# A fused attention and two-layer MoE kernel: token blocks of 512 in place of 384, and other places in SBUF for the buffers around them

## The chip, the cores and the metric

The kernel runs on one core of a Trainium2 chip. The metric is the device time of one execution in microseconds (us), taken as the median of several runs. Engines are named as the profile names them: PE is TensorE (PEld its weight loads), DVE is VectorE, ACT is ScalarE, POOL is GpSimd, SP is SyncE, which here issues every DMA; SPq, ACTq and so on are the engines' instruction queues.

## The reference

Three stages follow each other; their tensors come in as 64-bit or 32-bit floats, and the output is 32-bit. The MoE weights come in as 64-bit floats and are turned into 32-bit floats on the chip.

```python
# 1: chunked attention, q, k, v of 4 x 8 x 768 x 64, 8 memory keys per head
for c in range(nc):                      # chunks of 32 queries
    q_c = q[:, :, c_start:c_end]
    k_ctx = k[:, :, l_start:r_end]       # 16 keys to the left, 8 to the right
    k_full = np.concatenate([mem_k, k_ctx], axis=2)
    v_full = np.concatenate([mem_v, v_ctx], axis=2)
    scores = scale * np.matmul(q_c, k_full.transpose(0, 1, 3, 2))
    a = softmax(scores)
    out[:, :, c_start:c_end] = np.matmul(a, v_full)
x = out.transpose(0, 2, 1, 3).reshape(3072, 512)
# 2: first MoE, w_gate and w_val 512 x 1536, w_out 1536 x 512
x = (sigmoid(x @ w_gate) * (x @ w_val)) @ w_out
# 3: second MoE, w_in 512 x 2048, w_out 2048 x 512
h = x @ w_in
y = (h * sigmoid(1.702 * h)) @ w_out
```

## The kernel before

**Numbers as two halves.** Every matmul operand is split into a high part (rounded to the matmul's format) and a low part (the remainder), and each product is three matmuls: high by high, high by low, low by high. A weight slot `w` holds both parts of one unit of weights (128 x 2 x 512), and x is held as `xh` and `xl`.

**Blocks and phases.** The 3072 tokens go in 8 blocks of 384. Phase 1 runs the first MoE over each block: for each of 12 slices f of the hidden layer, `first_product` multiplies x by a gate slice (8 matmuls with the high weights, L694, and 4 with the low, L701), then by a value slice; `gated` makes the sigmoid on ACT (L718), the product on DVE (L721), and its high and low parts `gh` (ACT, L724) and `gl` (L728); `gemm2` multiplies them by an output slice into four PSUM banks Y (12 matmuls, L845). That is 36 matmuls, each 128 x 128 by 128 x 384, for a block and an f. The result goes to DRAM (`y_dram`) through two staging tiles and comes back for phase 2, the second MoE: per block and f of 16, 12 matmuls 384 wide (L694, L701) and 9 that are 512 wide (`gemm4` through `mm3`, L672), since there the weights are the moving operand and the output has 128 tokens a tile (3 tiles a block).

**Attention.** Each of 32 tiles covers 96 queries, so a block holds exactly four. The tiles of block 0 come first, the prologue, all PE-path (q, k and the probabilities are transposed on PE, L357, L365, L564; scores L474, values L625; evicted into `xh` by ACT, L635, and `xl` by DVE, L639); those of block 1 are PE-path tiles that run inside block 0, in one set of buffers `pa`; the others run inside the block before their own (`attention_b`), with transposes on DVE (L458 to L464, L599) from q and k that many small DMAs bring in (L283).

**Conversion.** One unit of 64-bit weights (512 KB) goes through `convert`: a DMA into a buffer `raw` (L240), ACT `rebias` (L244), DVE `rest` (L249), ACT `sign` (L254), DVE `join` (L257), ACT `high` (L262), POOL `low` (L266). 36 units belong to phase 1 and are converted during the prologue and block 0, 32 to phase 2 and are converted in slots of phase 1 as those come free, from block 7 on. There are 3 raw buffers, and 2 more for the first 16 units in the place of the second x block. 17 slots lie where the prologue's buffers were.

**Order.** `Schedule` lists every step with its engine, an assumed duration, what it reads and writes and a due time, and sets the order of the instructions of each engine by it; `clock` gives the matmuls' due times. On the chip each engine then works strictly in that order and waits at an instruction whose inputs are not there. PE has one gate bank G and one value bank V, so the gate product of f+1 cannot begin before ACT has read the sigmoid of f out of G.

Of the kernel before, what the change touches and what calls it, by code (L numbers as in the profile page):

```python
# [130 lines left out]
def kernel(  # L131
# [40 lines left out]
    clock = [20.0]  # L172
# [13 lines left out]
    NXR = 16  # L186
# [13 lines left out]
    def xkeys(i):  # L200
        return [("x", i, c) for c in range(BLK // TQ)]
# [25 lines left out]
    def convert(slot, src, late=False):  # L227
        u = nconv[0]
        nconv[0] += 1
        i = nraw[0]  # L230
# [793 lines left out]
```

## Time and profile before

| | us |
|---|---|
| median of 3 runs | 1271.63 (1267.9 to 1279.07) |
| the profiled execution | 1272.78 |
| its span, first to last instruction | 1270.9 |
| PE busy | 1225.8 (96%), 8320 matmuls |
| DVE, ACT, POOL busy | 612.1, 532.3, 219.4 |

The profiled execution is 1.9 us longer than its span. Busy time of PE is modelled from start to the end of the pipeline, so neighbouring matmuls overlap in it, and the time that a stream of matmuls takes is read from the distance of their starts.

### The profile page before, as it was taken

To read this page: it belongs to the slowest core of one execution; us is meant where nothing else is said; L and a number is where in the kernel's file an instruction comes from. 1 tells how busy PE (TensorE), PEld (TensorE's weight loads), DVE (VectorE), ACT (ScalarE), POOL (GpSimd) and SP (SyncE) were. 2 spreads that over 40 slices of the span, in tenths; PEclk is the share of its full clock that TensorE was granted. 3 is DMA by queue.
4 is the path that set the end of the run, shared out by engine and by line. 5 is a ranking of instruction groups with operands and counts; after the bars stand their busy time and mean duration, and the time that the engine had idled before them with its cause. 6 is when DMAs were issued, how large, how long until landed. Compare 5 with 4: busy or idle time off the path is not lost.

```text
span 1270.9 us, 20929 instructions
## 1 busy us (share of the span) xinstructions
PE 1225.8 (96%) x8320; PEld 1149.7 (90%) x8320; DVE 612.1 (48%) x1274; ACT 532.3 (42%) x902; POOL 219.4 (17%) x202
## 2 busy tenths in 40 slices
PE   5698899999999999999999999999999999999998
PEld 4688799899999999999999989999999999998997
DVE  6775757647738467385555631222222222222322
ACT  4998824333424234243358962323232322222222
POOL 3575600000000000000046662101010000001000
PEclk8899999999999999999999999999999999999999
DMA  9646433322303123021034520101010101010000
GB/s 189 181 140 181 136 57 66 64 82 44 71 15 52 47 40 72 12 48 49 18 104 165 176 91 1 50 1 50 1 50 1 50 1 38 13 36 15 26 1 26
DMA packets 173213, 78.04 MB, mean 61 GB/s; under 512 B 137659, under 2 KB 166587, under 8 KB 173115
## 3 DMA queue, kind: packets, MB, share of 16 engines
q1 hardware_dynamic: 173115, 76.71, 23.1%
q8 instruction: 65, 1.06, 0.3%
q14 instruction: 33, 0.27, 0.1%
HBM read 64.08 MB, written 12.58 MB: 60 GB/s over the span
## 4 chain that ended last, share of the span: by engine, by line
PE 77%; ACT 8%; SPq 4%; DMA 4%; DVE 4%; issue 2%; POOL 2%; ACTq 0%; DVEq 0%; POOLq 0%
PE bank L694 28%; PE bank L672 21%; PE bank L701 14%; PE bank L845 11%; SPq L283 4%; ACT raw L254 3%; ACT f L244 2%; PE bank L625 2%; DVE f L257 1%; DMA raw<-in_moe_w_val_dram 1%; DMA raw<-in_moe_w_out_dram 1%; PE bank L474 1%; POOL w L266 1%; DVE raw L249 1%; ACT w L262 1%
## 5 line engine op out<-in xcount | busy, mean ns | idle before, releaser
L694 PE MATMUL bank<-xh,w 128*128 128x384 f32 x1280 | 437.6, 342 | 20.6 <-ACT sig L718 14.2
L694 PE MATMUL bank<-xl,w 128*128 128x384 f32 x1280 | 434.6, 340 | 1.3 <-DVE xl L639 1.3
L721 DVE TENSOR_TENSOR sig<-bank,sig 128x384 f32<-128x384 f32 x224 | 124.4, 555 | 416.8 <-ACT sig L718 312.0
L701 PE MATMUL bank<-xh,w 128*128 128x384 f32 x1280 | 276.2, 338 | 0.4 <-POOL w L266 0.4
L718 ACT ACTIVATE sig<-bank 128x384 f32<-128x384 f32 x224 | 110.9, 495 | 387.4 <-PE bank L701 386.8
L694 PEld LDWEIGHTS bank<-xh,w 128*128 128x128 f32 x1280 | 243.8, 190 | 28.1 <-ACT sig L718 16.7
L694 PEld LDWEIGHTS bank<-xl,w 128*128 128x128 f32 x1280 | 244.1, 191 | 3.8 <-DVE xl L639 1.8
L672 PE MATMUL bank<-w,gh 128*128 128x512 f32 x768 | 239.2, 393 | 0.0
L701 PEld LDWEIGHTS bank<-xh,w 128*128 128x128 f32 x1280 | 227.1, 188 | 9.3 <-POOL w L266 0.7
L724 ACT ACTIVATE gh<-sig 128x384 fp32r<-128x384 f32 x224 | 117.7, 525 | 174.5 <-DVE sig L721 167.3
L845 PE MATMUL bank<-gh,w 128*128 128x384 f32 x768 | 166.2, 338 | 2.1 <-ACT f L868 1.6
L672 PEld LDWEIGHTS bank<-w,gh 128*128 128x128 f32 x768 | 142.1, 188 | 21.7
L672 PE MATMUL bank<-w,gl 128*128 128x512 f32 x384 | 151.3, 394 | 0.0
L728 DVE TENSOR_TENSOR gl<-sig,gh 128x384 fp32r<-128x384 f32 x184 | 104.2, 566 | 94.2 <-ACT gh L724 92.3
L845 PEld LDWEIGHTS bank<-gh,w 128*128 128x128 f32 x768 | 135.6, 188 | 4.5 <-ACT f L868 2.0
L266 POOL TENSOR_TENSOR w<-f,w 128x512 fp32r<-128x512 f32 x68 | 93.4, 1381 | 67.0 <-ACT w L262 63.9
L542 POOL TENSOR_TENSOR pn_b<-e,sm 96x448 f32<-96x448 f32 x24 | 23.2, 968 | 457.3 <-DVE sm L534 457.3
L894 POOL TENSOR_TENSOR xl<-f,xh 128x384 fp32r<-128x384 f32 x32 | 33.2, 1040 | 339.8 <-ACT xh L891 339.6
L254 ACT ACTIVATE raw<-raw 128x512 f16<-128x512 f32 x62 | 84.4, 1379 | 9.0 <-DVE raw L249 8.8
L672 PEld LDWEIGHTS bank<-w,gl 128*128 128x128 f32 x384 | 72.2, 188 | 17.2 <-DVE gl L728 0.3
L599 DVE STREAM_TRANSPOSE pt<-pn_b 32x256 f32<-32x256 f32 x192 | 83.6, 435 | 3.0
L845 PE MATMUL bank<-gl,w 128*128 128x384 f32 x384 | 82.5, 336 | 0.2 <-POOL gl L728 0.2
(79 smaller groups left out, 869.2 us busy)
## 6 DMA issues: line engine op xcount, KB each, us to landing
raw<-in_moe_w_out_dram SPq DMA_DIRECT2D x26, 512.0 KB
raw<-in_moe_w_in_dram SPq DMA_DIRECT2D x16, 512.0 KB
y_dram<-f SPq DMA_DIRECT2D x32, 192.0 KB
f<-y_dram SPq DMA_DIRECT2D x32, 192.0 KB
out_dram<-f SPq DMA_DIRECT2D x23, 256.0 KB
vn<-in_v_dram SPq DMA_DIRECT2D x24, 240.0 KB
raw<-in_moe_w_gate_dram SPq DMA_DIRECT2D x10, 512.0 KB
raw<-in_moe_w_val_dram SPq DMA_DIRECT2D x10, 512.0 KB
```

Of the source, the lines that this page charges most:

```text
L254: nc.scalar.activation(half[:, :, 1], words[:, :, 1].bitcast(F32), AF.Copy, scale=2.0**-60)
L266: nc.gpsimd.tensor_tensor(out=w[:, 1, :], in0=ft, in1=w[:, 0, :].bitcast(F32), op=ALU.subtract)
L283: add("sp", 0.45, lambda: nc.sync.dma_start(out=dst(), in_=src), r=list(r), w=[key], nbytes=n)
L599: nc.vector.transpose(T["pt"][r * CH : (r + 1) * CH, :, c * CH : (c + 1) * CH], T["pn"][c * CH : (c + 1) * CH, :, kb * CH : (kb + 1) * CH],)
L672: nc.tensor.matmul(ps_out, a, c, start=(first and i == 0 and j == 0), stop=(last and i == n - 1 and j == 2),)
L694: nc.tensor.matmul(bank[bk][:, :n], w[:, 0, ts[t]], x[xb][:, t, :n], start=t == 0 and x is xhs, stop=False)
L701: nc.tensor.matmul(bank[bk][:, :n], w[:, 1, ts[t]], xhs[xb][:, t, :n], start=False, stop=t == NK - 1)
L718: nc.scalar.activation(sig[:, :n], bank[src_sig][:, :n], AF.Sigmoid, scale=scale)
L721: nc.vector.tensor_tensor(out=sig[:, :n], in0=bank[src_val][:, :n], in1=sig[:, :n], op=ALU.mult)
L724: nc.scalar.activation(gh[:, :n], sig[:, :n], AF.Copy)
L728: eng.tensor_tensor(out=gl[:, :n], in0=sig[:, :n], in1=gh[:, :n].bitcast(F32), op=ALU.subtract)
L845: nc.tensor.matmul(bank[Y[m]][:, :n], w[:, wi, m * P : (m + 1) * P], g[:, :n], start=f == 0 and j == 0, stop=f == F1 - 1 and j == 2,)
```

## The change

Blocks have 512 tokens, so there are 6. A tile of 96 no longer divides a block: `tiles[b]` lists the tiles that begin in block b (6, 5, 5, 6, 5, 5), and a tile that lies in two blocks is evicted in two parts; of tiles 5 and 10 the second part is held back (`held_back`) until the next x block can be written. The prologue has 6 tiles in place of 4, block 0 carries 5 PE-path tiles in place of 4, and blocks 1 to 4 carry 21 in place of 24. Each matmul of phase 1, and each `first_product` of phase 2, is 512 wide; phase 1 has 36 x 12 x 6 matmuls in place of 36 x 12 x 8, phase 2 has 24 x 16 x 6 (all 512 wide) in place of 21 x 16 x 8, 4896 in place of 6144. Phase 2 uses 4 of 6 output banks for a block, in a ring, where it had two sets of 3.

In the conversion, every second unit's sign is made on DVE (`sign_dve`) and not on ACT. The first 8 units have 5 raw buffers (the two of the second x block), units 8 to 29 have 5 as well (two lie in slots that are filled last), then 3. 26 slots lie where the prologue was. The four slots filled last hold those two raw buffers and the buffers of `pa` first: units 34 and 35 (output slices 10 and 11) can be written only when the last PE-path tile, tile 10, has been transposed. `attention_b` has no buffers of its own: k lies in `raw0` and `raw1`, the unnormed probabilities in `raw2`, q and the memory keys in `f0` and `f1`, so its loads wait for the last conversions of block 0, and those of phase 2's weights wait for the last attention tile.

```diff
-    BLK = 384
-    blocks = [4] * 8
+    BLK = 512
+    NB = NT // BLK
+    tiles = [[t for t in range(NTILE) if t * TQ // BLK == b] for b in range(NB)]
+    NPRO = len(tiles[0])
+    NPE = NPRO + len(tiles[1])
...
-    clock = [20.0]
+    clock = [34.0]
...
-    NXR = 16
+    NXR = 8
+    NSR = 30
...
-    NLATE = 17
+    NLATE = 26
...
+        more = (NRAW, NRAW + 1) if u < NXR else (NRAW + 2, NRAW + 3) if u < NSR else ()
+        at = (*range(NRAW), *more)
+        i = at[nraw[0] % len(at)]
...
+        def sign_dve():
+            half = bits().bitcast(U16).rearrange("p (c w) -> p c w", w=4)
+            nc.vector.tensor_scalar(
+                out=half[:, :, 1], in0=half[:, :, 3], scalar1=0x8000, scalar2=None, op0=ALU.bitwise_and
+            )
...
-        add("act", c_act(512), sign, r=[kr], w=[kr2])
+        if u % 2:
+            add("dve", 0.9, sign_dve, r=[kr], w=[kr2])
+        else:
+            add("act", 1.4, sign, r=[kr], w=[kr2])
...
+            for i, blk in enumerate(sorted({c // NCH for c in g})):
+                if part not in (None, i):
+                    continue
+                cs = [c for c in g if c // NCH == blk]
+                a = (cs[0] - g[0]) * CH
+                m = len(cs) * CH
...
-            evict()
+            if t not in (NPRO - 1, NPE - 1):
+                evict()
+            else:
+
+                evict(0)
+                held_back.append(lambda: evict(1))
...
+        new_slots(late_pool[0], [u[1] for u in order[NW - NLATE : NW - 4]])
+        sraw.extend(spare(i, [P, 512], I64, f"raw_s{i}") for i in (3, 2))
+        t = spare(1, [P, 2, H, D], F32, "qkn_a")
+        pa.t.update(qn=t[:TQ, 0], kn=t[:, 1], pw=spare(0, [TQ, H, P], F32, "pw_a"))
...
+        kb = [blocks4(raw[i].bitcast(F32), 2 * NCK + 1) for i in range(2)]
+        qb = [blocks4(fts[i], NCK) for i in range(2)]
+        mn, mt = [fts[i][:, NP * TQ :].rearrange("p (a r) -> p a r", a=NP) for i in range(2)]
+        pn = raw[2].bitcast(F32)[:TQ, : H * 3 * CH].rearrange("s (h k) -> s h k", h=H)
...
+        if u == NW - 2:
+            add("none", 0.0, lambda: open_slots((1, 0)), w=named(pa) + ["ident_a", "pa"])
+            gate = "pa"
+        convert(s, src, gate)
+    conv_keys = bits_keys(range(NRAW)) + [("f", i) for i in range(NF)]
+    add("none", 0.0, open_pb, w=conv_keys + ["pb"])
...
-    O = [[Y[0], Y[1], Y[2]], [Y[3], A0, A1]]
+    ring6 = [*Y, A0, A1]
+    O = [[ring6[(TT * b + i) % 6] for i in range(TT)] for b in range(NB)]
...
+        if b == 0:
+            held_back.pop()()
```

Line numbers of the changed kernel differ (L694 becomes L726, L718 becomes L750, and so on). How the instructions stand is shown at three places.

**ACT in block 0**, some four units of conversion, before (L244 is `rebias`, L254 `sign`, L262 `high`, L724 `gh`):

```order
L244 ACTIVATE f3_80<-raw2_76 128x512
L254 ACTIVATE raw2_76<-raw2_76 128x512
L244 ACTIVATE f2_79<-raw0_74 128x512
L254 ACTIVATE raw0_74<-raw0_74 128x512
L262 ACTIVATE w15_107<-f1_78 128x512
L262 ACTIVATE w25_105<-f3_80 128x512
L724 ACTIVATE gh1_84<-sig1_82 128x384
L262 ACTIVATE w26_108<-f2_79 128x512
L254 ACTIVATE xh1_raw_89<-xh1_raw_89 128x512
```

and after (L257 is `rebias`, L267 `sign`, L281 `high`, L756 `gh`):

```order
L281 ACTIVATE w3_106<-f0_77 128x512
L257 ACTIVATE f1_78<-raw_s2_655 128x512
L267 ACTIVATE raw0_74<-raw0_74 128x512
L595 ACTIVATE pt_97<-bank2_68 128x384
L281 ACTIVATE w15_107<-f1_78 128x512
L257 ACTIVATE f2_79<-raw0_74 128x512
L756 ACTIVATE gh0_83<-sig0_81 128x512
L257 ACTIVATE f3_80<-raw1_75 128x512
L267 ACTIVATE raw2_76<-raw2_76 128x512
```

Before, a sign stands beside each `rebias`; after, every second unit has none on ACT.

**DVE at the end of block 0**, before, from the last x tile of block 1 (`xl1`, L639) to the transposes of the first `attention_b` tile (L461, L462):

```order
L639 TENSOR_TENSOR xl1_783<-bank3_69,xh1_782 128x4x96
L721 TENSOR_TENSOR sig1_82<-bank1_67,sig1_82 128x384
L257 SCALAR_TENSOR_TENSOR f0_77<-f0_77,raw0_74 128x512
L249 TENSOR_SCALAR raw1_75<-raw1_75 128x512
L257 SCALAR_TENSOR_TENSOR f1_78<-f1_78,raw1_75 128x512
L438 STREAM_TRANSPOSE mt_b_1498<-mn_b_1497 128x128
L721 TENSOR_TENSOR sig0_81<-bank1_67,sig0_81 128x384
L728 TENSOR_TENSOR gl0_85<-sig0_81,gh0_83 128x384
L866 COPY f3_80<-bank5_71 128x384
L721 TENSOR_TENSOR sig1_82<-bank1_67,sig1_82 128x384
L866 COPY f3_80<-bank7_73 128x384
L461 STREAM_TRANSPOSE kt_93<-kbkb_0_1494 128x12x32
```

and after (L593 is the copy of tile 10's probabilities, L482 to L485 and L479 the transposes and copies of the first `attention_b` tile from `raw1` and `f1`, L675 the eviction into `xl`, L753 the product with the sigmoid, L918 the eviction of the Y banks into the staging tile `f3`):

```order
L593 COPY pt_97<-bank3_69 128x384
L482 STREAM_TRANSPOSE kt_93<-raw1_75 128x12x32
L483 STREAM_TRANSPOSE kt_93<-raw1_75 128x12x32
L485 COPY kt_93<-f1_78 128x4x8 x3
L675 TENSOR_TENSOR xl1_725<-bank3_69,xh1_724 128x4x64
L675 TENSOR_TENSOR xl0_88<-bank3_69,xh0_87 128x4x32
L479 STREAM_TRANSPOSE qt_92<-f1_78 128x384
L753 TENSOR_TENSOR sig0_81<-bank1_67,sig0_81 128x512
L760 TENSOR_TENSOR gl0_85<-sig0_81,gh0_83 128x512
L918 COPY f3_80<-bank5_71 128x512
L918 COPY f3_80<-bank7_73 128x512
L753 TENSOR_TENSOR sig1_82<-bank1_67,sig1_82 128x512
```

The transposes from freshly loaded k and q have moved ahead of the last `xl` of block 1 and ahead of the Y evictions.

**SP at the same place**, before (L240 loads weights, L872 stores block 0's result):

```order
L240 DMA raw1_75<-in_moe2_w_out_dram 128x512
L283 DMA qbqb_0_1493<-in_q_dram 32x4x32 x3
L283 DMA mn_b_1497<-in_mem_k_dram 8x4x32 x4
L283 DMA kbkb_0_1494<-in_k_dram 32x6x32 x16
L283 DMA kbkb_0_1494<-in_k_dram 16x4x32
L872 DMA y_dram_65<-f2_79 128x384
```

and after (L253 loads weights, L924 stores):

```order
L253 DMA raw2_76<-in_moe_w_out_dram 128x512
L305 DMA vn_91<-in_v_dram 120x8x64
L305 DMA vn_91<-in_mem_v_dram 8x8x64
L305 DMA f1_78<-in_q_dram 32x4x32
L305 DMA f0_77<-in_mem_k_dram 8x4x32 x4
L305 DMA raw1_75<-in_k_dram 32x4x32 x16
L305 DMA f1_78<-in_q_dram 32x4x32 x11
L305 DMA raw0_74<-in_k_dram 32x7x32 x16
L305 DMA vn_91<-in_v_dram 120x8x64
L305 DMA f0_77<-in_q_dram 32x4x32 x10
L924 DMA y_dram_65<-f2_79 128x512
```

The first store of a block's result has moved from behind 17 k loads to behind two sets of 16 and two sets of q loads.

## Rows read from the trace of the kernel before

**Rows 1.** Busy time by stretches: start:end, length, busy us (instructions) per engine, PEclk, DMA.

```profile
0.00:35.90 35.90, 21.24 (x321) 17.86 (x321) 23.66 (x52) 17.95 (x37) 10.65 (x19) 0.81 0.82 174
13.50:36.20 22.70, 14.31 (x201) 11.96 (x200) 20.41 (x45) 12.49 (x24) 8.45 (x12) 0.70 0.71 183
35.90:155.70 119.80, 100.65 (x752) 92.76 (x753) 86.33 (x126) 112.15 (x166) 77.48 (x65) 0.93 0.57 166
155.70:650.30 494.60, 492.93 (x4131) 480.64 (x4131) 304.90 (x775) 172.09 (x283) 26.18 (x29) 1.00 0.23 48
650.30:731.90 81.60, 78.49 (x445) 76.62 (x444) 48.58 (x64) 69.72 (x104) 52.93 (x41) 1.00 0.53 174
731.90:1270.90 539.00, 532.52 (x2677) 481.82 (x2675) 148.64 (x259) 160.36 (x315) 52.20 (x50) 1.00 0.08 26
```

**Rows 2.** Instruction groups of PE from 35.9 to 155.7 us: count, busy, mean, idle before.

```profile
L694 PE MATMUL bank<-xh,w 128*128 128x384 f32 x100 | 39.3, 393 | 15.4 <-ACT sig L718 11.6 <-ACT w L262 3.8
L694 PE MATMUL bank<-xl,w 128*128 128x384 f32 x100 | 37.9, 379 | 1.3 <-DVE xl L639 1.3
L701 PE MATMUL bank<-xh,w 128*128 128x384 f32 x100 | 23.1, 355 | 0.4 <-POOL w L266 0.4
L845 PE MATMUL bank<-gh,w 128*128 128x384 f32 x88 | 18.9, 342 | 0.0
L845 PE MATMUL bank<-gl,w 128*128 128x384 f32 x44 | 9.7, 341 | 0.2 <-POOL gl L728 0.2
L564 PE MATMUL bank<-ident_a,pw_a 96*128 96x96 f32 x32 | 3.8, 268 | 1.8 <-POOL pw_a L542 1.8
L625 PE MATMUL bank<-pt,vn 128*64 128x96 f32 x64 | 3.5, 252 | 0.3 <-ACT pt L574 0.3
L474 PE MATMUL bank<-kt,qt 64*32 64x64 f32 x192 | 2.9, 221 | 1.1 <-ACT qt L372 1.1
L365 PE MATMUL bank<-ident_a,kn_a 128*128 128x128 f32 x16 | 2.4, 272 | 0.0
L357 PE MATMUL bank<-ident_a,qn_a 96*128 96x96 f32 x16 | 2.0, 245 | 0.0
```

**Rows 3.** Timeline of PE: start us, us, engine, line; three places in turn.

```profile
605.49 0.34 PE L694 MATMUL bank<-xh,w 128*128 128x384 f32 x1
...
611.73 0.34 PE L694 MATMUL bank<-xh,w 128*128 128x384 f32 x1
...
842.70 0.63 PE L672 MATMUL bank<-w,gh 128*128 128x512 f32 x2
...
844.78 0.51 PE L701 MATMUL bank<-xh,w 128*128 128x384 f32 x2
...
45.55 0.53 PE L694 MATMUL bank<-xh,w 128*128 128x384 f32 x1
45.87 0.53 PE L694 MATMUL bank<-xl,w 128*128 128x384 f32 x1
```

**Rows 4.** Conversion: groups of 35.9 to 155.7 us; L249's line view, ns min/median/max.

```profile
L254 ACT ACTIVATE raw<-raw 128x512 f16<-128x512 f32 x30 | 40.9, 1384 | 3.0 <-DVE raw L249 3.0
...
L249 DVE TENSOR_SCALAR raw<-raw 128x512 int32<-128x512 int32 x30 | 26.9, 904 | 7.1 <-DMA raw<-in_moe_w_gate_dram 2.5 <-DMA raw<-in_moe_w_val_dram 2.3 <-DMA raw<-in_moe_w_in_dram 2.1
...
L249 DVE TENSOR_SCALAR xh_raw<-xh_raw 128x512 int32<-128x512 int32 x3 | 3.9, 1301 | 0.0
...
L249 DVE TENSOR_SCALAR raw<-raw x62: 407/629/1974, 31.2 to 740.2; 128x512 int32<-128x512 int32 x62
```

**Rows 5.** Attention's groups on PE from 155.7 to 650.3 us, of 24 tiles.

```profile
L625 PE MATMUL bank<-pt,vn 128*64 128x96 f32 x384 | 21.1, 252 | 0.0
L474 PE MATMUL bank<-kt,qt 64*32 64x64 f32 x1152 | 17.7, 221 | 0.0
```

**Rows 6.** The first-product group of PE from 650.3 to 745 us.

```profile
L694 PE MATMUL bank<-xh,w 128*128 128x384 f32 x112 | 38.2, 341 | 5.3 <-ACT sig L718 2.7 <-DVE sig L721 2.6
```

**Rows 7.** Timeline of SP's queue at the start of block 1.

```profile
151.75 9.31 SPq L283 DMA_DIRECT2D kbkb<-in_k_dram  x17
161.49 0.83 SPq L872 DMA_DIRECT2D y_dram<-f  x2
```

More of the change, by code (lines that the diff above doesn't have):

```diff
@@ L795 @@
-    for i, (_, s, src) in enumerate(order[: NW - NLATE]):
-        convert(s, src)
-        if i == 0:
-            for t in range(NPRO):
-                attention(t, pro_bufs[t], pro_banks[t], True)
-    used = []
-    for x in pro_bufs:
-        for n in x.t:
-            used += [(x.k[n], i) for i in range(4)] + [x.k[n]]
-    add("none", 0.0, open_late, w=used + ["ident", "late"])
-    for _, s, src in order[NW - NLATE :]:
-        convert(s, src, True)
-    add("none", 0.0, open_x1, w=["x1"] + [k for i in range(2) for k in (("raw", NRAW + i), ("raw", NRAW + i, 2))])
@@ L808 @@
[L808 to L813 removed]
+        late_pool.append(ctx.enter_context(tc.tile_pool(name="cp2", bufs=1)))
+        new_slots(late_pool[0], [u[1] for u in order[NW - NLATE : NW - 4]])
+        sraw.extend(spare(i, [P, 512], I64, f"raw_s{i}") for i in (3, 2))
+        t = spare(1, [P, 2, H, D], F32, "qkn_a")
@@ new lines, in named, with bits_keys, attend @@
+    def named(bufs):
+        return [k for n in bufs.k for k in [(bufs.k[n], i) for i in range(4)] + [bufs.k[n]]]
+    def bits_keys(ids):
+        return [("raw", i, *x) for i in ids for x in ((), (2,))]
+    def attend(ts, bufs, banks):
+        for t in ts:
+            attention(t, bufs(t), banks(t), True)
+    gate = None
+    for u, (_, s, src) in enumerate(order):
+        if u == 1:
+            attend(tiles[0], lambda t: pro_bufs[t], lambda t: pro_banks[t])
+        if u == NXR:
+            add("none", 0.0, open_late, w=[k for x in pro_bufs for k in named(x)] + ["ident", "late"])
+            add("none", 0.0, open_x1, w=["x1"] + bits_keys((NRAW, NRAW + 1)))
+            held_back.pop()()
+            attend(tiles[1], lambda t: pa, lambda t: (A0, A1))
+            gate = "late"
+        if u == NW - 4:
+            add("none", 0.0, lambda: open_slots((3, 2)), w=["sraw"] + bits_keys((NRAW + 2, NRAW + 3)))
+            gate = "sraw"
+        if u == NW - 2:
+            add("none", 0.0, lambda: open_slots((1, 0)), w=named(pa) + ["ident_a", "pa"])
+            gate = "pa"
+        convert(s, src, gate)
@@ L831, in attention_b @@
     def attention_b(b):
-        for t in range(tile0[b], tile0[b] + blocks[b]):
+        for t in tiles[b]:
             first = t == NPE
@@ L896, in lo @@
                 )
-            add("sp", 0.45, load, r=[("y", m, NTB * b + i) for i in range(NTB)], w=[kst], nbytes=P * BLK * 4)
+            add("sp", 0.45, load, r=[("y", m, b)], w=[kst], nbytes=P * BLK * 4)
             add("act", c_act(BLK), hi, r=[kst], w=xkeys(xb))
@@ L927 @@
     freed.sort()
+    quads = range(0, P, CH)
+    done = [(f"kb{i}", r, p) for i in range(2) for r in quads for p in (0, 1, 2, 3, "edge")]
+    done += [(f"qb{i}", r, c) for i in range(2) for r in quads for c in range(NCK)]
+    done += [("mn", r) for r in quads] + ["mt", ("pn", 0), ("pn", 1), "pb"]
+    add("none", 0.0, lambda: None, w=done + conv_keys)
     slot_in2 = [freed[2 * f][1] for f in range(F2)]
```

128 lines of the change are left out of this document (58 added, 70 removed).

## The prediction

> **What bounds the kernel now.** I first cut the span at the places where the work changes and read the busy times by stretch [rows 1]: the prologue up to the first matmul of the first product (35.9 us), block 0 up to the end of block 1's first gate product (155.7), blocks 1 to 6 (650.3), the last block of phase 1 (731.9) and phase 2. From 155.7 on PE is busy for 492.9 of 494.6, 78.5 of 81.6 and 532.5 of 539.0 us: the other engines are covered there. Ahead of that it is not: 21.2 of 35.9 us in the prologue and 100.7 of 119.8 in block 0, at a mean granted clock of 0.81 and 0.93, while ACT is busy for 112.2 of the 119.8. So the kernel is PE for 1115 us, and ACT's conversion and DVE's attention for the first 156.
>
> In block 0 I counted what PE does [rows 2]: 432 matmuls of the products and four PE-path tiles, which together were busy for 14.6 us, 3.65 a tile (an upper bound, since neighbours overlap in it). The pace of a product matmul is read from starts [rows 3]: from 605.49 to 611.73 lie 36 of 384 columns, 173.3 ns each. So block 0 holds 432 x 0.1733 = 74.9 + 14.6 = 89.5 us of work in 119.8, and **30.3 us are lost**. The same rows give 20.5 us of idle time, of which 16.8 ended with ACT (15.4 ahead of the first product, 1.1 and 0.3 ahead of scores and values); the clock took 0.07 x 119.8 = 8.4, and some 1.4 is left for restarts.
>
> **The wider matmul itself: nothing.** From 842.70 to 844.78 lie 9 matmuls of 512 columns, 231.1 ns each; 231.1 / 173.3 = 1.333 is just 512 / 384 [rows 3]. At 45.55 us two of 384 columns are 0.32 us apart [rows 3], which is 384 / 1.2 GHz, the lower of the two clock levels, with nothing beside it. So the columns are paid, and the 1248 matmuls that fall away (6144 to 4896) were not paid singly. Phase 1 is 3456 x 0.1733 = 599 us before and 2592 x 0.2311 = 599 after; phase 2 is 1536 x 0.1733 + 1152 x 0.2311 = 532.4 before and 2304 x 0.2311 = 532.5 after. The Trainium skill, on the page "TensorE: Matmul & The Clock Gate", section "Back-to-back issue gap", has a gap of N / 2.4 + 2.5 ns when warm, a fixed 2.5 ns for each matmul. By it, as an estimate, 1248 fewer would save 3 us; the rows are 6.6 to 7.1% above its 162.5 and 215.8 ns and show no fixed part, so the sum takes none.
>
> **The prologue: +11.4 us.** It has six tiles in place of four. DVE sets its pace: 20.4 of 22.7 us busy from 13.5 to 36.2 [rows 1], for four tiles less the first maximum, with a few conversion steps among them. A tile costs 20.4 / 4 = 5.1 by busy time, 22.7 / 4 = 5.7 by elapsed time, and 35.9 / 4 = 9.0 if the opening loads counted for each; two more are 10.2 to 18 us. I take the elapsed 11.4, since loads of later tiles run beside earlier ones: first product at 47.3. The two more memsets lie in DVE's wait for the first loads.
>
> **Block 0: work 118.1 us, loss 7.4 in place of 30.3.** PE's work becomes 432 x 0.2311 = 99.8 + 5 x 3.65 = 18.3, together 118.1. Against that stands the supply:
> - ACT was busy for 112.2 us, 41.5 of it in 30 signs of 1384 ns [rows 4]. Half of these go: 20.8. The remaining 70.7 either stay or, at most, grow by a quarter with the fifth tile and with 512 columns: 91 to 109 us. Both ends are below 118.1, so ACT no longer bounds the block.
> - DVE was busy for 86.3 us [rows 1]. It gets 15 signs. No row shows that instruction; the nearest is L249, also one in-place operation on every second word of the same buffer, at 407 ns at least, 904 in the mean of this stretch, 1974 at most [rows 4]. The signs cost 6 to 30 us; I take the mean, 13.6. With the rest unchanged or, without L249's 26.9, a quarter larger, DVE comes to 100 to 115 us: also below 118.1, though not by much.
> - Raw buffers are five in place of three for units 16 to 29, so DVE's 7.1 us of waiting for weights [rows 4] shrinks; that is cover, not gain.
>
> With ACT below PE, I let the 16.8 us of waits that ended with ACT go and keep the other 3.7; the clock's loss was 8.4 for 20.5 us of idle time, so 3.7 leave 1.7. To this come 2 us at the end of the block, which did not stand there before: DVE now has the transposes of freshly loaded k ahead of the last `xl` of block 1, and 17 such loads took SP 9.3 us to issue [rows 7]. By the order they begin when the last value slice's low part is done on POOL, some 50 product matmuls ahead of the end (11.6 us), and land about when DVE comes to them. The sum is 3.7 + 1.7 + 2 = 7.4; the bounds are 2 and the present 30.3. Block 1's first gate product ends at 47.3 + 118.1 + 7.4 = **172.8** in place of 155.7.
>
> **The rest: 1115.2 us becomes 1082.3.** Block 0 has done 512 tokens and not 384, so phase 1 has 2160 matmuls of 0.2311 left in place of 3024 of 0.1733: 499.2 for 524.1, -24.9. Three attention tiles fewer are left, each (21.1 + 17.7) / 24 = 1.6 us on PE [rows 5]: -4.9. In the turn to phase 2 PE waited 5.3 us [rows 6], on ACT and DVE busy with the second conversion (ACT 69.7 of 81.6 us [rows 1]). A block and its weights' slots now last a third longer for the same 32 units, and ACT has half the signs; I take 3 of the 5.3 off, with 0 and 5.3 as ends. Phase 2 stays, and so does the tail. The output ring costs nothing: the banks of `gemm4` that come round again are its third and fourth, and a first product stands between. The split tiles add a few evictions to ACT and DVE, which are idle more than a third of the time in these blocks [rows 1].
>
> Together 172.8 + 1115.2 - 24.9 - 4.9 - 3.0 = 1255.2 us of span. The profiled execution was 1.9 longer than its span, so 1257.1, against 1272.8 for that execution and a median of 1271.6: **1257 us**, 1.1% faster. About 1%, 12.7 us, is what a measurement of this kernel can tell from no change.
>
> **The rivals.**
> - *A wait takes the place of the one removed.* The hand-over from block 0 to block 1. Both Y staging tiles are stored only after 16 + 11 + 16 + 10 k and q loads in SP's queue, where 17 stood ahead before; at 9.3 / 17 = 0.55 us each that is 29 us and not 9.3 [rows 7]. DVE stands at its second Y eviction until the first store is over, and block 1's first value products queue behind it. PE's order has some 84 product matmuls (19 us) between tile 10 and the first instruction that needs the Y banks, and the stores land some 32 us after the k loads begin, which themselves begin 12 us before. That is even, with 0 to 10 us of stall if the loads start late; with the prologue at 9.0 us a tile the two give up to 16 more: 1263 to 1273, I say 1267, no change by the bound above. For it: the queue is full and in order. Against: the loads can start early where DVE is ahead.
> - *DVE becomes the bound.* POOL's work and L249 get in each other's way: the mean moves from 407 at best to 1301 for three of them [rows 4]. The Trainium skill, on the page "SBUF — State Buffer", section "Who interferes with whom", says that DVE in a two-port mode and POOL take a shared pair of ports in turn, for a whole instruction, and that the loser waits. The trace agrees in that one and the same instruction has 407 and 1974 ns; the price here is from these rows. 45 such instructions in block 0 (30 and 15) at 1.64 us, midway from 1301 to 1974, add 0.74 x 45 = 33 to DVE's mean of 107: 140, so block 0 loses 22 + 7.4 and the time is 1279, **slower** than before. It decides from a DVE total of 118 + 14.6 = 133 us, 1.48 us a piece. Against: the mean of 904 was measured with POOL busy for 77 of 119.8 us, and POOL's own load grows little.
> - *Matmuls have a fixed part after all.* If the 13.3 ns that 384 columns take beyond 384 / 2.4 were a matmul's own, 1248 fewer would save 16.6: 1240. The pace of 512 columns speaks against it, but was read where the activations are the stationary operand.
> - *The edit does less than it says*: ACT's order stays the bound (its waits on single instructions, table loads among them, and not its total). Then half of the 30.3 stays: 1265.
>
> **How the numbers follow.** The forecast with its own spread (1247 to 1266: the prologue from -1 to +5, the loss from 2 to 15, the turn's 3 either way) gets 0.56; the hand-over 0.17; the smaller effect 0.09; the fixed part 0.10; DVE 0.08. The hand-over and the smaller effect overlap with the forecast's upper end. The range of 1240 to 1274 reaches to the fixed part below and over the no-change cases above, and leaves out DVE's 0.08 and a little at either side. Faster than 1259 by this: a little over 0.7 of the forecast (0.41) and the fixed part (0.10), 0.51; slower than 1284: the upper part of the DVE case, 0.05; within 1%: 0.44.
>
> **What the profile would show.** Product matmuls 231 ns apart (right) or 225 and less (the fixed part). The first product at 46 to 50 us. ACT's busy share of block 0 at 75 to 92%, with PE's waits on ACT under 5 us in all. The new sign on DVE at 0.8 to 1.0 us. Block 1's first gate product ending at 168 to 180. No PE wait over 3 us between 172 and 300, or the hand-over is at work. I am wrong if PE still waits more than 15 us in block 0, or if a wait appears in blocks 1 to 5 that none of these names.

## The result and the profile after

| | before | after |
|---|---|---|
| median of 7 runs each, us | 1272.26 (1267.86 to 1279.07) | 1261.28 (1258.15 to 1264.35) |
| ratio | 1 | 0.9912, 95% interval 0.9882 to 0.9941 |
| the profiled execution, its span | 1272.78, 1270.9 | 1264.35, 1262.6 |
| PE busy, matmuls | 1225.8, 8320 | 1231.8, 7120 |

The kernel became 0.9% faster. The interval does not reach a ratio of 1, but the gain lies just within the 1% that the prediction took as the least that can be told from it; 1257 us was forecast, just beyond it, in a range of 1240 to 1274. The profiled execution of the changed kernel is the slowest of its seven, 3.1 us above their median, so the traces show 8.4 us of the 11.0 that the medians gained. The busy times by stretch, with the columns of [rows 1], cut at the first matmul of the first product, at the sigmoid of block 1's first slice, at that of the last block and at that of phase 2:

```profile
0.00:49.17 49.17, 32.00 (x481) 26.52 (x481) 37.56 (x79) 23.54 (x51) 14.22 (x23) 0.85 0.68 146
49.17:182.01 132.84, 123.43 (x830) 97.42 (x831) 109.27 (x159) 99.38 (x155) 84.96 (x70) 0.95 0.58 154
182.01:625.96 443.95, 443.69 (x3094) 353.38 (x3093) 265.51 (x645) 146.69 (x221) 25.97 (x24) 1.00 0.23 49
625.96:723.77 97.81, 97.81 (x421) 78.52 (x420) 72.40 (x87) 68.02 (x102) 62.08 (x44) 1.00 0.52 160
723.77:1262.60 538.83, 534.92 (x2301) 431.88 (x2299) 135.47 (x192) 137.41 (x228) 48.76 (x39) 1.00 0.07 24
```

The shape of [rows 1] is kept. PE is covered from block 1 on, and now in the turn too: in the last block it is busy for all of 97.81 us. Only the prologue and block 0 are not PE's. The prologue is 13.3 us longer. Block 0 holds about as many product matmuls (427 for 432), each a third wider, and took 12 us more, with ACT at 99.4 of 132.8 us (113.1 of 120.8 before, cut in the same way) and DVE at 109.3.

PE's groups in block 0 (49.17 to 181.75 us), which answer to [rows 2]:

```profile
L726 PE MATMUL bank<-xh,w 128*128 128x512 f32 x100 | 42.0, 420 | 2.0 <-ACT w L281 2.0
...
L733 PE MATMUL bank<-xh,w 128*128 128x512 f32 x100 | 28.8, 413 | 0.0
L897 PE MATMUL bank<-gh,w 128*128 128x512 f32 x88 | 25.8, 417 | 0.0
...
L585 PE MATMUL bank<-ident_a,pw_a 96*128 96x96 f32 x40 | 4.9, 273 | 6.2 <-POOL pw_a L563 6.2
L645 PE MATMUL bank<-pt,vn 128*64 128x96 f32 x80 | 4.4, 252 | 3.2 <-ACT w L281 1.6 <-ACT pt L595 1.5
```

The 11.6 us of waits on the sigmoid are gone. The 2.0 us ahead of L726 end with the first matmul of the block and so lie in the prologue:

```profile
49.17 0.79 PE L726 MATMUL bank<-xh,w 128*128 128x512 f32 x1 [2.04 <-ACT w L281]
```

That leaves 9.4 us of idle time in block 0 (PE's 123.43 of 132.84 us above say the same), all of it ahead of the transposes and values of PE-path tiles. With the 427 product matmuls that begin before 181.75 at 233.3 ns (read below) and five tiles that were busy for 18.6 us in all, work is 118.2 us of the 132.6, so 14.4 are lost where 30.3 were. The idle time is not the whole loss, as the timeline of PE around one such wait and the windows beside it show:

```profile
72.17 1.09 PE L897 MATMUL bank<-gh,w 128*128 128x512 f32 x4
75.06 1.30 PE L585 MATMUL bank<-ident_a,pw_a 96*128 96x96 f32 x8 [1.79 <-POOL pw_a L563]
76.06 2.06 PE L733 MATMUL bank<-xh,w 128*128 128x512 f32 x4
77.92 1.48 PE L897 MATMUL bank<-gh,w 128*128 128x512 f32 x4
```

```profile
49.17:55.30 6.13, 6.13 (x15) 4.83 (x16) 6.10 (x7) 4.01 (x6) 4.21 (x3) 0.53 1.14 283
...
75.70:79.10 3.40, 3.40 (x13) 2.77 (x12) 1.50 (x3) 1.81 (x4) 3.40 (x4) 0.55 0.55 154
...
133.70:137.10 3.40, 3.40 (x11) 2.68 (x10) 3.16 (x2) 3.12 (x5) 3.40 (x4) 0.55 0.15 50
```

PE stood idle for 1.79 us until 75.06; from 75.7 the granted clock is down to near its lower level for 3.4 us, and four matmuls of L733 take 77.92 - 76.06 = 1.86 us, 465 ns each. It fell twice like that (the second time after a wait of 3.2 us, the longest), and block 0 also began with 6.1 us at 0.53: 0.45 x 6.8 + 0.47 x 6.1 = 6 us.

The pace, that is the distance of neighbouring starts, in phase 2 (as in [rows 3]):

```profile
1004.61 0.39 PE L726 MATMUL bank<-xh,w 128*128 128x512 f32 x1
...
1006.48 0.63 PE L704 MATMUL bank<-w,gh 128*128 128x512 f32 x2
```

Eight first-product matmuls in 1.87 us are 233.3 ns each (from the starts in nanoseconds; those shown are rounded); phase 1 has the same distance (642.52, 642.75, 642.99 and so on).

The conversion in block 0 (as in [rows 4]; L267 is the sign on ACT, L262 `rest`, L271 the sign on DVE), ACT first, then DVE:

```profile
L267 ACT ACTIVATE raw<-raw 128x512 f16<-128x512 f32 x10 | 13.7, 1371 | 0.0
```

```profile
L262 DVE TENSOR_SCALAR raw<-raw 128x512 int32<-128x512 int32 x21 | 17.6, 844 | 5.6 <-DMA raw<-in_moe_w_out_dram 5.1 <-DMA raw<-in_moe_w_val_dram 0.6
L262 DVE TENSOR_SCALAR raw_s<-raw_s 128x512 int32<-128x512 int32 x10 | 12.9, 1290 | 0.0
L271 DVE TENSOR_SCALAR raw<-raw 128x512 uint16<-128x512 uint16 x11 | 12.1, 1097 | 0.1
...
L271 DVE TENSOR_SCALAR raw_s<-raw_s 128x512 uint16<-128x512 uint16 x5 | 5.7, 1139 | 0.1
```

And the hand-over to block 1, in DVE's and SP's timelines:

```profile
189.96 0.69 DVE L918 COPY f<-bank 128x512 f32<-128x512 f32 x1 [1.11 <-PE bank L897]
196.57 0.69 DVE L918 COPY f<-bank 128x512 f32<-128x512 f32 x1 [5.92 <-DMA y_dram<-f]
```

```profile
188.37 4.81 SPq L305 DMA_DIRECT2D f<-in_q_dram  x10
193.29 0.84 SPq L924 DMA_DIRECT2D y_dram<-f  x2
```

The wait that the first rival described is there: the store is issued behind the k and q loads, and DVE stands at its second Y eviction for 5.9 us. But PE's longest wait between 175 and 300 us is 1.2 us, so it stayed covered.

### The profile page after: what moved, and what is told of

It reads as the page before. It is cut to its first block, busy times and chain, and to the rows that moved or that the text cites. A ratio compares the mean times of both kernels' runs of the same rounds, so it can differ in the third digit from the quotient of the medians.

```text
span 1262.6 us, 18066 instructions
## 1 busy us (share of the span) xinstructions
PE 1231.8 (98%) x7120; PEld 987.7 (78%) x7120; DVE 620.2 (49%) x1161; ACT 475.0 (38%) x754; POOL 236.0 (19%) x198
## 4 chain that ended last, share of the span: by engine, by line
PE 90%; DVE 5%; DMA 1%; ACT 1%; issue 1%; POOL 1%; SPq 1%; DVEq 0%; POOLq 0%; ACTq 0%
PE bank L726 33%; PE bank L704 21%; PE bank L733 17%; PE bank L897 14%; PE bank L645 2%; PE bank L495 1%; DVE f L276 1%; DVE pw L563 1%; SPq L305 1%; POOL pw_a L563 1%; PE bank L585 0%; DVE raw_s L262 0%; DVE raw L271 0%; DVE raw L262 0%; DVE sm L552 0%
## 5 line engine op out<-in xcount | busy, mean ns | idle before, releaser
L726 PE MATMUL bank<-xh,w 128*128 128x512 f32 x960 | 382.4, 398 | 2.3 <-ACT w L281 2.0
L726 PE MATMUL bank<-xl,w 128*128 128x512 f32 x960 | 380.9, 397 | 0.0
L753 DVE TENSOR_TENSOR sig<-bank,sig 128x512 f32<-128x512 f32 x168 | 115.9, 690 | 434.1 <-ACT sig L750 337.3
L733 PE MATMUL bank<-xh,w 128*128 128x512 f32 x960 | 264.1, 398 | 0.0
L750 ACT ACTIVATE sig<-bank 128x512 f32<-128x512 f32 x168 | 100.6, 599 | 389.6 <-PE bank L733 389.3
L726 PEld LDWEIGHTS bank<-xh,w 128*128 128x128 f32 x960 | 181.5, 189 | 47.9 <-ACT w L281 2.3
L726 PEld LDWEIGHTS bank<-xl,w 128*128 128x128 f32 x960 | 181.5, 189 | 43.3
L733 PEld LDWEIGHTS bank<-xh,w 128*128 128x128 f32 x960 | 179.3, 188 | 42.8
L756 ACT ACTIVATE gh<-sig 128x512 fp32r<-128x512 f32 x168 | 106.2, 632 | 197.4 <-DVE sig L753 190.3
L897 PE MATMUL bank<-gh,w 128*128 128x512 f32 x576 | 159.6, 399 | 0.0
L760 DVE TENSOR_TENSOR gl<-sig,gh 128x512 fp32r<-128x512 f32 x128 | 91.0, 711 | 74.5 <-ACT gh L756 74.2
L897 PE MATMUL bank<-gl,w 128*128 128x512 f32 x288 | 79.7, 398 | 0.0
L620 DVE STREAM_TRANSPOSE pt<-raw 32x256 f32<-32x256 f32 x168 | 73.1, 435 | 2.6
```

What stands on the lines that cost most here:

```text
L620: nc.vector.transpose(T["pt"][r * CH : (r + 1) * CH, :, c * CH : (c + 1) * CH], T["pn"][c * CH : (c + 1) * CH, :, kb * CH : (kb + 1) * CH],)
L726: nc.tensor.matmul(bank[bk][:, :n], w[:, 0, ts[t]], x[xb][:, t, :n], start=t == 0 and x is xhs, stop=False)
L733: nc.tensor.matmul(bank[bk][:, :n], w[:, 1, ts[t]], xhs[xb][:, t, :n], start=False, stop=t == NK - 1)
L750: nc.scalar.activation(sig[:, :n], bank[src_sig][:, :n], AF.Sigmoid, scale=scale)
L753: nc.vector.tensor_tensor(out=sig[:, :n], in0=bank[src_val][:, :n], in1=sig[:, :n], op=ALU.mult)
L756: nc.scalar.activation(gh[:, :n], sig[:, :n], AF.Copy)
```

## The experiments

One table holds what the readings rest on. Block 0 and its loss come from the one profiled execution of each kernel. Block 0 is counted from the first product to the start of block 1's first sigmoid (0.3 to 0.9 us later than above); its loss is that length less PE's work of 89.5 us (blocks of 384) or 118.2 (512). Times are medians; ratios are to the kernel before, timed beside it (its medians were 1271.3 to 1271.9).

| kernel | signs on DVE | first product | block 0 | loss | time, us | ratio, 95% interval |
|---|---|---|---|---|---|---|
| 384 (before) | none | 35.9 | 120.8 | 31 | 1271.3 to 1272.3 | |
| 384, half signs | half | 36.6 | 118.6 | 29 | 1269.06 | 0.9973, 0.9952 to 0.9995 |
| the same, order by measured durations | half | 36.3 | 121.9 | 32 | 1268.84 | 0.998, 0.9963 to 0.9998 |
| 384, those signs dropped | none, half missing | 36.9 | 109.7 | 20 | 1257.4 | 0.9891, 0.9853 to 0.993 |
| 384, half signs, POOL's low part cut | half | 37.0 | 107.1 | 18 | 1255.79 | 0.9883, 0.984 to 0.9926 |
| 512, all signs on ACT | none | 47.4 | 140.3 | 22 | 1272.64 | 0.9997, 0.998 to 1.0014 |
| 512 (after) | half | 49.2 | 132.8 | 15 | 1261.28 | 0.9912, 0.9882 to 0.9941 |
| 512, 3 raw buffers | half | 49.4 | 129.7 | 12 | 1259.18 | 0.9889, 0.9867 to 0.991 |
| 512, order by measured durations | half | 49.4 | 131.6 | 13 | 1260.82 | 0.9913, 0.9885 to 0.9941 |
| 512, norms on DVE | half | 48.0 | 136.6 | 18 | 1264.16 | 0.9939, 0.9916 to 0.9961 |
| 512, DVE signs dropped | none, half missing | 48.3 | 131.2 | 13 | 1257.28 | 0.9882, 0.9861 to 0.9902 |
| 512, 3 raw buffers, a third | third | 48.6 | 133.1 | 15 | 1262.32 | 0.992, 0.9902 to 0.9938 |
| 512, 3 raw buffers, measured durations | half | 49.1 | 133.5 | 15 | 1261.75 | 0.992, 0.9903 to 0.9937 |

### The parts, each alone

All signs on ACT, in blocks of 512:

```diff
-        if u % 2:
-            add("dve", 0.9, sign_dve, r=[kr], w=[kr2])
-        else:
-            add("act", 1.4, sign, r=[kr], w=[kr2])
+        add("act", c_act(512), sign, r=[kr], w=[kr2])
```

> The changed kernel with every sign on ACT again. Theory (ACT's relief made the gain): ACT's busy time in block 0 goes from 99.4 to 99.4 + 15 x 1.38 = 120 us, above the 118.2 us of work that PE has there, so block 0's loss goes from 14.4 back to 25 to 30 us, with waits on ACT's sigmoid again, and the hand-over to phase 2 waits again: 1272 to 1281 us. Rival (the wider block made the gain, a third more matmuls beside the same conversions): PE's 118 us still cover ACT, the loss stays below 18 us and the time within 4 us of the changed kernel, 1258 to 1265 us.

1272.64 us: without the signs on DVE the change brings nothing. Its block 0, by window and PE group (line numbers 3 lower):

```profile
47.35:187.69 140.34, 126.15 (x830) 98.34 (x831) 99.99 (x142) 116.84 (x173) 79.97 (x70) 0.94 0.56 147
```

```profile
L723 PE MATMUL bank<-xh,w 128*128 128x512 f32 x100 | 42.4, 424 | 3.8 <-ACT w L281 2.3 <-ACT sig L747 1.5
...
L582 PE MATMUL bank<-ident_a,pw_a 96*128 96x96 f32 x40 | 5.5, 293 | 7.1 <-POOL pw_a L560 7.1
```

The time came to where the theory put it, but not by its steps. ACT came to 116.8 us, 3 below what was worked out and just below PE's 118.2, and the loss of 22 lies below the 25 to 30. PE's waits on the sigmoid came back with 1.5 us ahead of L723 (the 2.3 on `w` beside them end with the block's first matmul), while the longest, 7.1 us, is on POOL's norm; and in the turn to phase 2 PE waited 0.8 us in all. So the wider blocks cover the turn without the signs on DVE, and how ACT's load makes the loss is argued from its total.

Half the signs on DVE, in blocks of 384 (the kernel before, with the function `sign_dve` added):

```diff
-        add("act", c_act(512), sign, r=[kr], w=[kr2])
+        if u % 2:
+            add("dve", 0.9, sign_dve, r=[kr], w=[kr2])
+        else:
+            add("act", 1.4, sign, r=[kr], w=[kr2])
```

> The kernel before, blocks of 384, with every second sign on DVE and nothing else. Theory: ACT's 112.2 us in block 0 become about 91, the loss of 30.3 us about half of that, and the wait of 5.3 us in the turn to phase 2 goes: 1272 - 15 - 5 = 1252 us, 1245 to 1258, which would be faster than the changed kernel, because 384 columns are paid at 0.4513 ns and not at 0.4557. Rival (the wider block made the gain): with 89.5 us of PE work ACT's 91 and DVE's 86 + 15 still do not fit, the loss stays at 25 us or more, 1264 to 1274 us.

1269.06 us. The theory falls: ACT's relief alone brings 3 us, not 20, and of the turn's wait 2.5 us stay. DVE's groups and the window of its block 0:

```profile
36.60:155.21 118.61, 100.38 (x754) 92.34 (x755) 105.56 (x141) 91.47 (x147) 81.10 (x67) 0.92 0.56 166
```

```profile
L250 DVE TENSOR_SCALAR raw<-raw 128x512 int32<-128x512 int32 x29 | 27.2, 944 | 6.5 <-DMA raw<-in_moe_w_gate_dram 4.2 <-DMA raw<-in_moe_w_out_dram 2.3
...
L259 DVE TENSOR_SCALAR raw<-raw 128x512 uint16<-128x512 uint16 x15 | 18.9, 1263 | 0.3
```

ACT went from 113.1 to 91.5 us, DVE from 86.3 to 105.6, and the block became only 2 us shorter. So the engine that was short may only have changed.

### What holds the narrow block

The same kernel without the signs on DVE:

```diff
         if u % 2:
-            add("dve", 0.9, sign_dve, r=[kr], w=[kr2])
+            pass
```

> Blocks of 384 with every second sign on ACT and the others left out altogether (weights of these units lose their sign). The theory that ACT's relief alone made the gain has fallen with the half signs on 384 columns. New theory: at 384 columns moving signs from ACT to DVE only moves the bound, DVE was busy for 105.6 of block 0's 118.6 us there; without the 17 signs of 1.3 us it has 83, ACT 91, PE 89.5 us of work, and block 0 falls to 102 to 108 us, the time to 1253 to 1260 us. Rival (the order, with PE-path tiles that come due before POOL has normed them, holds block 0): 115 us or more, 1265 to 1270 us.

```profile
36.88:146.56 109.68, 97.31 (x754) 89.50 (x755) 85.81 (x124) 92.28 (x147) 76.76 (x65) 0.95 0.63 178
```

1257.4 us, inside the new theory's range; DVE fell by 19.8 us and the block by 8.9, less than the 11 to 17 that were expected of it. And with DVE's instructions made shorter in place of fewer, by taking work from POOL:

```diff
-    nc.gpsimd.tensor_tensor(out=w[:, 1, :], in0=ft, in1=w[:, 0, :].bitcast(F32), op=ALU.subtract)
+    nc.gpsimd.tensor_tensor(out=w[:, 1, :P], in0=ft[:, :P], in1=w[:, 0, :P].bitcast(F32), op=ALU.subtract)
```

> Blocks of 384 with half the signs on DVE, and POOL's low part of a weight made for 128 of 512 columns only (the products with low weights use those, or the high part, in place of the rest). Theory (POOL and DVE hold each other up, which makes DVE's part of the conversion long): L250 falls from 944 to about 450 ns, the DVE sign from 1263 to about 750, DVE's busy time in block 0 from 105.6 to 75 to 85 us, block 0 from 118.6 to 100 to 106 us, the time to 1250 to 1258 us. Rival (DVE's long durations come from elsewhere, from the loads into the same buffers or from ACT on them): they stay above 850 and 1100 ns, and the time at 1264 us or more.

```profile
36.99:144.13 107.14, 96.35 (x754) 89.69 (x755) 84.45 (x143) 91.22 (x148) 49.38 (x67) 0.95 0.61 184
```

```profile
L250 DVE TENSOR_SCALAR raw<-raw 128x512 int32<-128x512 int32 x29 | 18.3, 637 | 10.1 <-DMA raw<-in_moe_w_gate_dram 5.0 <-DMA raw<-in_moe_w_val_dram 2.7 <-DMA raw<-in_moe_w_out_dram 2.4
L259 DVE TENSOR_SCALAR raw<-raw 128x512 uint16<-128x512 uint16 x15 | 15.4, 1026 | 0.3
```

1255.79 us. No DVE instruction was taken away, yet DVE's busy time fell by 21.1 us and the block by 11.5: the means went from 944 to 637 and from 1263 to 1026 ns, about half of the way that was expected. Both runs fit a DVE that is short at 384 columns with half signs, and the second fits that a part of its time is POOL's doing. Neither shows it alone: dropping a sign and cutting POOL's part also shorten the chain from a load to a ready slot, so not all of the 8.9 and 11.5 need be DVE's; and both blocks stayed longer than the 108 and 106 us that their theories allowed.

The rival for the narrow block was its order, so it was planned again from measured durations (`rebias`, `high` and `low` likewise):

```diff
-        add("dve", 0.45, rest, r=[kr], w=[kr2])
+        add("dve", 0.95, rest, r=[kr], w=[kr2])
...
-            add("dve", 0.9, sign_dve, r=[kr], w=[kr2])
+            add("dve", 1.25, sign_dve, r=[kr], w=[kr2])
```

> Blocks of 384 with half the signs on DVE, and the order made from durations as measured there: rest 0.95 us, sign on DVE 1.25, rebias 0.68, high 0.64, low on POOL 1.42. Theory (the width is needed: at 384 columns PE has 89.5 us of work in block 0 and DVE is short whatever the order): block 0 stays at 112 us or more, the time at 1263 to 1270 us. Rival (the half signs were only badly ordered among blocks of 384, and the width does nothing for the gain): block 0 falls below 106 us, the time to 1252 to 1258 us, as fast as the changed kernel or faster.

```profile
36.33:158.26 121.93, 102.33 (x746) 93.86 (x747) 96.73 (x142) 91.46 (x147) 78.48 (x62) 0.90 0.51 158
```

1268.84 us: this other order does not help; whether yet another would, no run tells. It shows one thing more. With the new order DVE was busy for 96.7 us and not 105.6, with as many instructions (the mean of L250 fell from 944 to 779 ns, with POOL's work as it was), and ACT for 91.5. Neither fills the 121.9 us, and 32 us were lost all the same. So the totals of ACT and DVE do not say alone how long the narrow block is; what does is open.

### What is left in the wide block

Three raw buffers from unit 8 on:

```diff
-    NSR = 30
+    NSR = 8
...
-            add("none", 0.0, lambda: open_slots((3, 2)), w=["sraw"] + bits_keys((NRAW + 2, NRAW + 3)))
+            add("none", 0.0, lambda: open_slots((3, 2)), r=["late"], w=["sraw"] + bits_keys((NRAW + 2, NRAW + 3)))
```

> The changed kernel with 3 raw buffers from unit 8 on, where it has 5 up to unit 29. Theory: the buffers are cover only; DVE waits a few us longer for weights, the loss of block 0 moves by 0 to 4 us: 1261 to 1265 us. Rival (the two further buffers made the gain, since the conversion was held up by loads): the loss goes up by 10 us or more, 1271 us and above.

```profile
49.41:179.15 129.74, 119.05 (x830) 92.99 (x831) 112.33 (x153) 99.27 (x155) 84.10 (x70) 1.00 0.59 155
```

1259.18 us, below both expectations: the two further buffers bring nothing. The clock is 1.00 here, where the changed kernel has 0.95 over the same block, while PE's idle time is 10.7 us against 9.4. So the 3 us between the two blocks are the clock's and not the waits'; the intervals of the two ratios overlap, and which kernel is faster is not settled.

The order from measured durations (the edit as at 384, with 1.15 for the sign):

> The changed kernel with the order made from durations as measured in block 0: rest 0.95 us in place of 0.45, sign on DVE 1.15 in place of 0.9, rebias 0.68 and high 0.65 in place of 0.56, low on POOL 1.42 in place of 1.33. Theory (what is left of block 0's loss, 14.4 us, comes from PE-path tiles placed before their softmax and norm are done, since the order believes DVE faster than it is): the waits on POOL's norm and on the probabilities, 6.2 and 3.2 us, fall below 4 together, 1255 to 1259 us. Rival (it is the engines' capacity and not the order): within 2 us of the changed kernel, 1259 to 1264 us.

1260.82 us; the wait on POOL's norm went only from 6.2 to 5.4 us. The rival's time holds, and this order is not what is left. The two norms of each PE-path tile on DVE (for the prologue's tiles the third, which alone was POOL's):

```diff
-            en = ["dve", "dve" if early else "pool", "pool"]
+            en = ["dve", "dve", "dve"]
```

> The changed kernel with the two norms that POOL makes of each PE-path tile in block 0 (1.36 us each, 10 of them) on DVE, as the first chunk of each tile is (0.77 us). Theory (POOL's queue holds PE's transposes up): PE's wait of 6.2 us on the normed probabilities falls below 2, POOL has 13.6 us less and DVE 7.7 us more in block 0: 1256 to 1259 us. Rival (DVE is the one that is short, 109 of 132.6 us busy): other waits grow by as much, 1261 to 1268 us.

1264.16 us, and the wait ahead of the transposes did not go but grew, on another engine:

```profile
L585 PE MATMUL bank<-ident_a,pw_a 96*128 96x96 f32 x40 | 4.9, 274 | 9.7 <-DVE pw_a L563 9.7
```

So taking the norm out of POOL's queue does not make it earlier. The DVE signs dropped:

> The changed kernel with the DVE signs left out altogether (weights of these units lose their sign). DVE's 109 us in block 0 become about 90. Theory (DVE is what is still short in block 0 of the changed kernel, where 14.4 us are lost): the loss falls to 6 to 9 us, the time to 1253 to 1257 us. Rival (what is left is the chain of a PE-path tile, softmax, norm, transposes, whose length does not hang on DVE's load): the loss stays at 12 us or more, 1258 to 1263 us.

```profile
48.25:179.45 131.20, 121.61 (x830) 95.32 (x831) 97.07 (x142) 99.72 (x156) 85.23 (x71) 0.97 0.59 155
```

```profile
L726 PE MATMUL bank<-xh,w 128*128 128x512 f32 x100 | 41.9, 419 | 3.7 <-ACT sig L750 2.8 <-ACT w L281 0.9
...
L585 PE MATMUL bank<-ident_a,pw_a 96*128 96x96 f32 x40 | 4.2, 249 | 2.4 <-POOL pw_a L563 2.3
```

DVE has 12 us less, the loss is 13 in place of 15 and PE's idle time 9.6 us in place of 9.4: in the wide block DVE is not what is short. The time of 1257.28 us lies at the edge between both expectations, and by block 0 the rival holds. The waits change place with every edit (POOL's norm 2.3 us here, the sigmoid 2.8), while their sum does not: of the wide blocks with half the signs on ACT, the three whose windows are shown have 9.4 to 10.7 us of idle time. No run took work from POOL in the wide block, or more than half the signs from ACT, so these two supplies were not tried.

Two attempts at a better kernel, a third of the signs on DVE and the measured durations, both with 3 raw buffers:

```diff
-        if u % 2:
+        if u % 3 == 1:
```

> The changed kernel with 3 raw buffers from unit 8 on and every third sign on DVE in place of every second. ACT has 99 + 5 x 1.37 = 106 us in block 0, DVE 112 - 5 x 1.4 = 105. Theory (both are short, and the best share makes them equal): block 0 is 127 to 130 us as with half, 1257 to 1261 us in all. Rival (ACT is the one that PE waits for first, as with all signs on it): the loss grows by a third of the 7.5 us between the half and none, 1262 to 1265 us.

> The changed kernel with 3 raw buffers from unit 8 on and the order made from durations as measured. Theory (the two add up where they do anything): 1257 to 1260 us, not to be told from 3 raw buffers alone, since the order brought nothing with 5. Rival (with fewer buffers the loads come later, and an order that knows DVE's pace is worth more): 1252 to 1256 us.

1262.32 and 1261.75 us. Neither beats half the signs with 3 raw buffers. A third is where its rival put it, though ACT (106.6 us) and DVE (103.7) came out as worked out. The other lies above what its theory and its rival expected, so neither holds.

### The width of a matmul

```diff
-            first_product(slot_in2[f], xb, BLK, hb)
+            first_product(slot_in2[f], xb, BLK, hb, m=(512, 480, 448, 384, 320, 256)[b])
```

> The changed kernel with the first product of phase 2 cut to 512, 480, 448, 384, 320 and 256 columns in its six blocks; the remaining columns of these products are not computed. Read from starts of neighbouring matmuls. If each column of the changed kernel costs 0.4557 ns whatever the width: 218.7, 204.2, 175.0, 145.8, 116.7 ns. If only 512 columns carry the price and narrower ones go at 0.4513: 216.6, 202.2, 173.3, 144.4, 115.5. With a fixed part of 2.5 ns for each matmul the step from 512 to 256 would be 233.3 to 117.9.

Eight matmuls of a first product with 480, 448, 384, 320 and 256 columns, the first of them and what follows the last:

```profile
847.86 0.38 PE L727 MATMUL bank<-xh,w 128*128 128x480 f32 x1
...
849.60 0.63 PE L704 MATMUL bank<-w,gh 128*128 128x512 f32 x2
...
940.31 0.37 PE L727 MATMUL bank<-xh,w 128*128 128x448 f32 x1
...
941.93 0.63 PE L704 MATMUL bank<-w,gh 128*128 128x512 f32 x2
...
1025.80 0.34 PE L727 MATMUL bank<-xh,w 128*128 128x384 f32 x1
...
1027.21 0.87 PE L734 MATMUL bank<-xh,w 128*128 128x384 f32 x4
...
1082.48 0.31 PE L727 MATMUL bank<-xh,w 128*128 128x320 f32 x1
...
1083.65 0.62 PE L704 MATMUL bank<-w,gh 128*128 128x512 f32 x2
...
1153.38 0.28 PE L727 MATMUL bank<-xh,w 128*128 128x256 f32 x1
...
1154.33 0.63 PE L704 MATMUL bank<-w,gh 128*128 128x512 f32 x2
```

That is 1.74 / 8 = 217.5, then 202.5, 176.3, 146.3 and 118.8 ns. Over all 16 slices of a block the medians of such eights are 216.3, 202.0, 176.4, 146.6 and 117.8 ns, and 233.3 at 512, or 0.451, 0.451, 0.459, 0.458, 0.460 and 0.456 ns a column. None of the three expectations fits. The widths of 448 and 480 go at the 0.451 of the kernel before, and 256 to 384 cost more a column than 512 does; a fixed part of 2.5 ns would fit 512, 320 and 256, but not 480 (218.9) and 448 (204.5). So 512 columns carry no price of their own, and why the same kind of matmul goes at paces that differ by 2% no run tells.

## Why the prediction was right

The sum was 1255.2 us of span and 1262.6 were measured, so of the 15.7 us that were forecast between the profiled executions about half, 8.3, came; the medians are kinder. The direction and the mechanism held, one term was too small:

- **The first product**: 47.3 forecast, 49.2 measured. Two tiles cost 13.3 us and not 11.4, between the elapsed price and the upper bound, and DVE, which was to set the pace there, was busy for 13.9 us more.
- **Block 0** is where the time was mis-sized: a loss of 14.4 us for the forecast 7.4. The mechanism stood: the waits on the sigmoid went, ACT came to 99.4 (forecast 91 to 109), DVE to 109.3 (100 to 115), its sign to 1.15 us in the mean of 17 for the 0.904 taken. What failed is the step that kept 3.7 us of other waits and 1.7 of clock and added 2 for the end of the block: with the sigmoid's waits gone, 9.4 us of others stood ahead of the PE-path tiles (6.2 on the norm, 3.2 ahead of the values), and the clock cost about 6. Shorter DVE work, another order and another engine for the norm each left a loss of 13 to 18 us, so none of these three is the whole of it; the cause stays open. The prediction had also read the loss before a little wrong: 1.4 of its 20.5 us of idle time, and of the 16.8 that ended with ACT, lie ahead of the block's first matmul,

```profile
35.89 0.44 PE L694 MATMUL bank<-xh,w 128*128 128x384 f32 x1 [1.37 <-ACT w L262]
```

so the block had 19.1 us of idle time, and restarts and the rest took 2.8 and not 1.4.

- **The rest** was 1080.9 us for the forecast 1082.3. The turn's wait went altogether (5.3 us and not 3), and the slower matmuls of phase 1 took about 2160 x 0.0022 = 4.8 back; with both the rest would be 1084.8, so a further 3.9 us were gained that no term names, and the near match is partly luck. "The wider matmul itself: nothing" was taken from matmuls of phase 2 with the activations stationary, at 231.1 ns; the products of phase 1 took 233.3. Phase 2 as a whole is 538.8 for 539.0.
- **The rivals.** The hand-over was at work for 5.9 us on DVE, with cover. DVE did not bind in the wide block: 1.06 us was the mean of its 50 `rest` and signs, not the 1.48 from which it would decide. A fixed part of 13.3 ns is excluded: 512 columns would take 226.6 ns and took 233.3. The Trainium skill, on the page "SBUF — State Buffer", section "Who interferes with whom", has DVE in a two-port mode and POOL take a shared pair of ports in turn. The traces of the narrow block agree in that DVE's means fell, by 307 and 237 ns, when POOL had 32 us less to do; but another order alone took 165 ns off L250, and the longest L250 with half the signs, 4.0 us, is longer than any POOL instruction in that block (2.5 us), so waiting for one such instruction is not the whole of it.
- **The signs named.** Four held: the first product at 49.2 us, matmuls not at 225 ns, PE's waits on ACT in block 0 at 3.1 us, and no PE wait over 1.2 us between 175 and 300. Three were missed, each by a little: ACT's share of 74.8%, DVE's sign, and the end of block 1's first gate product at 181.8 us for 168 to 180.

What the prediction did not ask is which part makes the gain. Neither does alone: half the signs on DVE brought 3 us at 384 columns, the wider block 0 us with all signs on ACT, both together 11. The ledger of spans shows where the rest came from. At half signs, from 384 to 512, the first product comes 12.6 us later and block 0 is 14.2 longer, but what follows up to phase 2 falls from 573.3 to 541.8; the block takes in 28.7 us more of PE's work, and 14.5 of its loss are filled. That left 3.8 us in the profiled executions and 7.8 in the medians. Why this is so is argued and not shown. At 384 columns the block is some 120 us long whichever engine makes the signs, with ACT at 113 us or DVE at 106, both above PE's 89.5; at 512 PE's own 118 us are longer than what either engine has, but with all signs ACT (116.8) is near that length, and the loss of 22 eats what the width could give. Against it stands the narrow block in the order from measured durations, which stayed long with both engines below 97 us. And the width came with the other places of the buffers, which no run takes apart but for the raw buffers.

## What to carry to other kernels

When several engines feed PE, compare each engine's busy time in the stretch with PE's work there, after the change and for each part of it alone: here, moving signs from ACT to DVE brought 3 us while PE had less work in the stretch than either engine, and 11 where PE's own work outlasted both. Take the comparison as a guide only, since one order left 32 us unused with neither ACT nor DVE full. When the largest wait is taken away, do not keep the smaller ones at their old size; price them as the next in line, and add what the clock loses behind each.

## What the runs showed of the hardware

The same DVE instruction (L250, 128 x 512) took 371 ns at least, 552 in the median and 3996 at most in the 384 kernel with half signs; with POOL's work cut, 377, 430 and 1840. An idle time of 1.79 us on PE was followed, some 0.6 us after work had begun again, by 3.4 us at 0.55 of the clock, near the lower of its two levels (1.2 GHz); the two together are 1.79 + 0.45 x 3.4 = 3.3 us, almost twice the wait. First products of one width differ by up to 2% in pace: 384 columns took 173.3 ns in phase 1 of the kernel before, 174.5 in its phase 2 and 176.4 in the kernel with changed widths.
